# A scan-plus-FFN kernel on one core: the 64-bit weights' last bits copied as 16-bit words, and another order of work on ScalarE and SyncE

## The chip, the core and the metric

The program runs on one core of a Trainium2 chip. The core has five engines, each with its own in-order queue: TensorE (PE in the profile, its weight loads PEld), VectorE (DVE), ScalarE (ACT), GpSimd (POOL) and SyncE (SP), which here issues all DMAs. They wait for each other through semaphores. The metric is the device time of one execution in microseconds (us), lower is better.

## The reference

Two stages follow one another. The first is a chunked linear attention over 4 batches, 8 heads, 768 positions, head width 32 and state width 16; its result of 3072 tokens by 256 goes through a bilinear feed-forward stage:

```python
log_a = np.log(np.clip(a, 1e-06, 1.0))
for c in range(nc):
    cum = np.cumsum(la, axis=-1)
    L = np.exp(cum[:, :, :, None] - cum[:, :, None, :]) * causal
    M = np.einsum('bhin,bhjn->bhij', Cc, Bc) * L
    y = np.einsum('bhij,bhjd->bhid', M, xc) + np.einsum('bhin,bhnd->bhid', Cc, state) * np.exp(cum)[..., None]
    state = decay_full * state + np.sum(Bx, axis=2)
...
a = x @ w1
b = x @ w2
h = a * b @ w3
return (h @ w_out).astype(np.float32)
```

x, a, B and C are float32. The four weight matrices w1, w2 (256 x 1024), w3 (1024 x 1024) and w_out (1024 x 256) come as float64, and the kernel must turn them into float32 itself.

## The kernel before

**Tiling.** The 768 positions are cut into 16 chunks of 48 (c0 to c15) and 8 slabs of two chunks (0 to 7); a slab holds 2 x 48 positions of 4 batches, which is 384 tokens. A chunk's steps are: loads `.T`, `.X`, `.K` and `sN.N`; `D0`, `D1` (the exponents' differences as matrix products), `E0`, `E1` (exp on ACT), `B0`, `B1` (weighting B, on POOL), `C` (C times B, 16 products), `M0` to `M3` (times the decay, on DVE), `Y` (32 small products, output and new state), `Z` and `x0` to `x3` (the state is transposed and copied into the next chunk's operand XE), `h` (ACT writes the high part of the output into XT) and `l` (DVE writes the remainder). From chunk 2 on the differences need cumulative sums that are computed once, written to DRAM by `a.save` and read back by each chunk's `.K`.

**Feed-forward.** w3 and w_out are first multiplied with each other, so that only two products per slab remain. For slab s and column block f (0 to 7) `ls.f.0` and `ls.f.1` are the two products x w1 and x w2, six matmuls of 384 columns each. `ls.f.a` copies the first from its PSUM bank into the gate buffer (ACT), `ls.f.g` multiplies the second in (DVE), `ls.f.h` casts the product to its high part (ACT), and `ls.f.l` subtracts for the low part (POOL or DVE). `zs.0` to `zs.2` are the products down to 256 columns, 24 matmuls of 256 columns each, and `ys.k` copies them out (ACT), `ys.kd` stores them (SP). High and low parts live in the buffer G, a ring of 9 column blocks: a cast into a block waits until the products of the slab before have read it. G shares its memory with the words' buffers below, so no cast runs before the last weight word is used.

**Words.** A weight block w0 to w7 (w1 and w2), o0 to o3 (w_out), v0 to v15 (w3) takes these steps: `.D` loads 512 KB of float64 into `st` (4 buffers), `.A` scales the high word into `mag` (6 buffers), `.Y` copies the low word's top bits over the high word's last bits, which `.A` has already read, `.L` shifts those bits down and keeps them with the sign, `.S` shifts `mag` up and sets them in. For w blocks `.H` and `.P` split the result into a high and a low part, for v blocks `.M` multiplies it with w_out (8 matmul records), and `eN.a`, `eN.b` split the sum for a pair of column blocks.

**Order.** Nothing is scheduled by the compiler: the string PLAN names every step in program order, and each engine runs its own steps in that order. A letter behind a colon picks the engine (a, v or p). `+5` puts in five matmuls of zeros on PE, which compute nothing. Up to slab 2 the column products share three PSUM banks in turn (bank 4, 5, 6), from then on four (bank 4 to 7); `pl_bank` assigns them by the table ORDER, which the change leaves alone.

Of the kernel before, what the change touches and what calls it, by code (L numbers as in the profile page):

```python
# [30 lines left out]
k.I b.m01:v k.X c1.X b.m10:v c0.D0 b.m11:v w2.D k.L1 c0.D1 c0.E0 a.scan c2.T k.R0 a.t0:p w3.D c1.D0 c0.E1 a.r0:p  # L31
w0.A:a k.R1 c0.B0 c1.D1 s1.N c1.E0 c0.B1 c0.M0 c0.M1 c1.B0 c0.M2 c1.E1 c0.M3 w0.Y:v +1 c0.Y c1.B1 a.t1:p w0.L
c1.C a.r1:p c0.Z c0.x0:v c0.x1:a a.save c0.x2:v c0.x3:a c2.X c1.M0 c0.h c1.M1 c1.M2 w1.A:a c1.M3 w0.S +6 c1.Y
w1.Y:a w0.H:v w4.D w0.P:v c1.h c0.l w2.A:a c1.l +5 l0.0.0 w2.Y:a w1.L w1.S l0.0.1 c2.K w1.H:v l0.0.a w3.A:a
w1.P:v c3.T +1 l0.1.0 c3.X c1.Z w3.Y:a w2.L w5.D l0.1.1 w2.S c3.K c1.x0:a c1.x1:v c2.D0 c1.x2:a c1.x3:v c2.D1
w2.H:v c2.E0 w6.D w2.P:v c2.E1 c2.B0 l0.1.a c2.B1 +3 c2.C l0.0.g w4.A:a l0.2.0 c2.M0 w4.Y:a c2.M1 c2.M2 c2.M3
w3.L c2.Y w3.S l0.2.a w5.A:a l0.2.1 w3.H:v w7.D w5.Y:a w3.P:v c3.D0 c3.D1 c4.T l0.1.g l0.3.1 c4.K c2.Z c3.E0
w4.L c2.h c3.B0 l0.3.0 s2.N c3.E1 c2.l c4.X c2.x0:a c3.B1 w4.S c3.C c2.x1:a c2.x2:a c2.x3:v o0.D c3.M0 l0.3.a
c3.M1 w6.A:a c3.M2 c3.M3 w4.H:v c3.Y w6.Y:a w4.P:v l0.4.1 l0.2.g w7.A:a w5.L l0.4.0 w5.S w7.Y:a w5.H:v o1.D
c4.D0 c4.D1 w5.P:v c5.T l0.4.a c5.K o0.A:a l0.3.g l0.5.1 c3.Z o0.Y:a l0.4.g l0.5.0 c5.X w6.L w6.S c3.h l0.5.a  # L40
c3.l o2.D l1.0.0 w6.H:v o1.A:a w6.P:v l1.0.1 l1.0.a l0.5.g o1.Y:a l1.0.g l0.6.0 w7.L c4.E0 o0.L l0.6.1 l0.6.a
c4.B0 w7.S c4.E1 l1.1.0 w7.H:v o3.D o2.A:a c4.B1 o0.S w7.P:p o2.Y:a l1.1.1 l0.6.g v0.D o1.L l0.7.0 o1.S l1.1.a
c3.x0:a l1.1.g v1.D l0.7.1 l0.7.a o2.L c3.x1:a o2.S c3.x2:a l1.2.0 o3.A:a l0.7.g v2.D c3.x3:v l1.2.1 l1.2.a
o3.Y:v v0.A:a l1.3.0 o3.L v0.Y:v l1.3.1 l1.3.a v0.L v1.A:a v0.S c4.C v1.Y:a o3.S v4.D v0.M c4.M0 v3.D c4.M1
# [12 lines left out]
c7.M3 l2.5.1 l2.5.a e3.b c8.T l0.7.l:p l1.0.h c8.K c7.Y l2.5.g l1.0.l:p l2.6.0 c7.Z c7.x0:v c7.h c7.x1:v l2.6.1
l2.6.a c7.l c7.x2:a c7.x3:v l2.7.0 l2.6.g s4.N l2.7.1 l2.7.a c8.X z0.0 l2.7.g z0.1 y0.0 y0.0d c9.T c9.K z0.2
y0.1 l2.0.h y0.1d l1.1.h l2.0.l:p l1.2.h l1.1.l:v l1.3.h l1.2.l:p l1.4.h l1.3.l:v c8.D0 l1.5.h c8.D1 l1.4.l:p
l1.6.h l1.5.l:v l1.7.h l1.6.l:p y0.2 l1.7.l:v c9.X c8.E0 l3.0.0:4 c8.E1 y0.2d c8.B0 c8.B1 z1.0 l3.0.a z1.1 y1.0  # L60
y1.0d z1.2 y1.1 y1.1d l2.1.h l2.2.h l2.1.l:p l2.3.h l2.2.l:v l2.4.h l2.3.l:p l3.0.1:4 l2.4.l:v y1.2 l2.5.h y1.2d
l2.6.h l2.5.l:p c8.C l3.0.g l2.7.h l2.6.l:v l3.1.0:4 l3.0.h l2.7.l:p c8.M0 c8.M1 l3.1.1:4 c8.M2 l3.1.a l3.0.l:p
c8.M3 c10.T l3.2.0:4 l3.1.g c10.K l3.2.1:4 l3.2.a c8.Y l3.2.g l3.3.0:4 c8.Z c8.x0:v c8.h c8.x1:v s5.N l3.3.1:4
l3.3.a c8.l c8.x2:a c8.x3:v l3.4.0:4 l3.3.g c10.X c9.D0 c9.D1 c9.E0 l3.4.1:4 c9.E1 c9.B0 l3.4.a c9.B1 c9.C
l3.4.g l3.5.0:4 c9.M0 c9.M1 c9.M2 c9.M3 l3.5.1:4 l3.5.a c11.T l3.6.0:4 l3.5.g c11.K l3.6.1:4 l3.6.a c9.Y l3.6.g
l3.7.0:4 c9.Z c9.x0:v c9.h c9.x1:v l3.7.1:4 l3.7.a c9.l c9.x2:a c9.x3:v z2.0 l3.7.g c11.X z2.1 y2.0 y2.0d z2.2
y2.1 y2.1d l3.1.h l3.2.h l3.1.l:p l3.3.h l3.2.l:v l3.4.h l3.3.l:p l4.0.0:4 l3.4.l:v y2.2 l3.5.h y2.2d l3.5.l:p
c10.D0 l4.0.a c10.D1 l4.0.1:4 c10.E0 c10.E1 c10.B0 l3.6.h c10.B1 c10.C l4.0.g l3.7.h l3.6.l:p l4.1.0:4 c10.M0
# [24 lines left out]
"""


@with_exitstack
def kernel(
    ctx: ExitStack,
    tc: tile.TileContext,
# [21 lines left out]
    nc = tc.nc  # L121
# [29 lines left out]
    def ins(i):  # L151
        return tc.keep_in_program_order(i) if ordered[0] else i
# [298 lines left out]
    def from_f64(name, loads, dst=None):  # L451
# [5 lines left out]
        v = {}  # L457
# [18 lines left out]

        @task(name + ".Y")
        def _(e):
            b = v["st"].bitcast(U8).rearrange("p (k e) -> p k e", e=8)
            copy(e, b[:, :, 4], b[:, :, 3])  # L480

        @task(name + ".L")
        def _(e):
            w = v["wh"].bitcast(I32)
            ins(nc.vector.tensor_scalar(w, w, 5, 7 - 2 ** 31, ALU.arith_shift_right, ALU.bitwise_and))  # L485
# [210 lines left out]
```

## Time and profile before

| | us |
|---|---|
| device time, median of 3 runs | 299.51 (299.01 to 301.11) |
| profiled execution, device time | 297.72 |
| profiled execution, span on the core | 296.0 |
| mean granted TensorE clock | 0.994 |
| DVE busy (317 instructions) | 155.5 |
| ACT busy (280) | 145.5 |
| POOL busy (105) | 68.6 |

Busy times overlap, so they say how much an engine did and not what the end waits for. PE is busy through nearly the whole span, so what counts is where PE stands still. The span has these stages: up to about 18 us the first loads and chunks 0 and 1; to 58 us the conversion of w1, w2 and w_out beside slab 0 and the first columns of slab 1; to 117 us the w3 blocks and the columns of slabs 1 and 2; at 116.8 us the first product down, z0; from then on, slab after slab, columns and products down. In the timelines the tile names are those of the code without their buffer numbers.

### The profile page before, as it was taken

Reading aid. Unit: us, or ns where it says so; the run is one execution under the profiler, and the core shown is the slowest. Engines: PE = TensorE matmul, PEld = TensorE weight load, DVE = VectorE, ACT = ScalarE, POOL = GpSimd, SP = SyncE. Lnnn points to the kernel's source line nnn. Section 1 sums busy time; section 2 is a strip of 40 time slices with the busy share of each in tenths; the row PEclk is TensorE's granted clock in tenths of the full one; section 3 lists DMA queues with packets and bytes.
Section 4 is the critical chain, followed back from the end, with each engine's and each line's share of the span. In section 5 each row is a group of like instructions: output and inputs, shape, how many; then the busy total and the mean of one; then the engine's idle time right before and its main releaser. Section 6 shows DMA issues by size and latency. Waiting matters only on the chain.

```text
span 296.0 us, 7543 instructions
## 1 busy us (share of the span) xinstructions
PE 281.7 (95%) x3076; PEld 254.3 (86%) x3080; DVE 155.5 (53%) x317; ACT 145.5 (49%) x280; POOL 68.6 (23%) x105
## 2 busy tenths in 40 slices
PE   8979869999999999959999999999999999999994
PEld 3467769888998999959999999999999999999994
DVE  4789959898775264062654355435543552332040
ACT  4589868688775283163442444244424441442241
POOL 8501003010001073082410341034103410340060
PEclk9999999999999999979999999999999999999999
DMA  5987865759881000311320132113211000100021
GB/s 160 332 230 232 217 219 166 251 169 295 282 268 49 27 2 2 89 39 38 102 73 29 41 97 77 29 38 99 76 29 37 20 2 2 35 20 0 18 56 36
DMA packets 22818, 29.47 MB, mean 100 GB/s; under 512 B 5530, under 2 KB 13056, under 8 KB 22784
## 3 DMA queue, kind: packets, MB, share of 16 engines
q1 hardware_dynamic: 22784, 29.00, 33.3%
q8 instruction: 24, 0.39, 0.6%
q14 instruction: 10, 0.08, 0.1%
HBM read 25.54 MB, written 3.29 MB: 97 GB/s over the span
## 4 chain that ended last, share of the span: by engine, by line
PE 89%; ACT 4%; DMA 2%; issue 1%; POOL 1%; DVE 1%; POOLq 0%; ACTq 0%; DVEq 0%
PE bank L155 89%; DMA st<-in_w_out_dram 2%; ACT g L161 1%; ACT st L161 1%; POOL g L164 1%; ACT mag L472 0%; POOLq L691 0%; ACT rr L387 0%; ACT xe L161 0%; DVE mag L491 0%; ACT ob L161 0%; ACT gf L161 0%; DVE st L485 0%; DVE rr L164 0%; ACT xt L161 0%
## 5 line engine op out<-in xcount | busy, mean ns | idle before, releaser
L155 PE MATMUL bank<-xt,w 128*128 128x384 f32 x768 | 148.6, 344 | 6.2 <-ACT ob L161 3.4
L155 PEld LDWEIGHTS bank<-xt,w 128*128 128x128 f32 x768 | 133.1, 189 | 11.2 <-ACT ob L161 3.7
L155 PE MATMUL bank<-woh,g 128*128 128x256 f32 x384 | 69.7, 281 | 0.3 <-POOL g L164 0.3
L164 POOL TENSOR_TENSOR g<-gf,g 128x384 fp32r<-128x384 f32 x40 | 44.1, 1124 | 110.7 <-PE bank L155 50.7
L164 DVE TENSOR_TENSOR gf<-gf,bank 128x384 f32<-128x384 f32 x64 | 35.3, 552 | 51.5 <-PE bank L155 43.3
L155 PEld LDWEIGHTS bank<-woh,g 128*128 128x128 f32 x384 | 59.6, 189 | 0.5 <-POOL g L164 0.5
L164 DVE TENSOR_TENSOR g<-gf,g 128x384 fp32r<-128x384 f32 x24 | 27.3, 1169 | 52.1 <-PE bank L155 30.7
L155 PE MATMUL bank<-wol,g 128*128 128x256 f32 x192 | 53.8, 280 | 0.0
L161 ACT COPY gf<-bank 128x384 f32<-128x384 f32 x64 | 31.4, 491 | 41.9 <-PE bank L155 41.7
L164 POOL TENSOR_TENSOR rr<-bn,rr 128x128 f32<-128x128 f32 x32 | 14.2, 458 | 105.0 <-ACT rr L387 62.9
L155 PEld LDWEIGHTS bank<-wol,g 128*128 128x128 f32 x192 | 36.4, 189 | 0.0
L161 ACT COPY ob<-bank 128x256 f32<-128x256 f32 x24 | 8.9, 372 | 50.8 <-PE bank L155 35.8
L161 ACT CAST g<-gf 128x384 fp32r<-128x384 f32 x64 | 29.0, 515 | 7.1 <-PE bank L155 6.4
L161 ACT COPY st<-st 128x512 uint8<-128x512 uint8 x22 | 30.3, 1376 | 0.6
L155 PE MATMUL bank<-wof,mag 128*128 128x256 f32 x128 | 29.7, 381 | 0.3 <-issue 0.2
L155 PEld LDWEIGHTS bank<-wof,mag 128*128 128x128 f32 x128 | 24.0, 190 | 3.5 <-DVE mag L491 0.4
L472 ACT ACTIVATE mag<-st 128x512 f32<-128x512 f32 x27 | 18.6, 688 | 10.0 <-DMA st<-in_w3t_dram 5.3
L155 PEld LDWEIGHTS bank<-rr,xe 64*32 64x32 f32 x1024 | 15.4, 107 | 7.3 <-issue 4.6
L155 PE MATMUL bank<-rr,xe 64*32 64x64 f32 x1024 | 18.5, 218 | 2.2 <-issue 1.5
L164 DVE TENSOR_TENSOR rr<-bank,rr 128x192 f32<-128x192 f32 x64 | 18.4, 349 | 2.0 <-POOL rr L164 1.5
L161 ACT CAST xt<-bank 128x384 fp32r<-128x384 f32 x16 | 7.8, 489 | 23.4 <-DVE zz L430 20.7
L387 ACT ACTIVATE rr<-bank 128x384 f32<-128x384 f32 x32 | 14.7, 502 | 8.6 <-PE bank L155 8.5
(57 smaller groups left out, 150.5 us busy)
## 6 DMA issues: line engine op xcount, KB each, us to landing
st<-in_w3t_dram SPq DMA_DIRECT2D x16, 512.0 KB
st<-in_w_dram SPq DMA_DIRECT2D x16, 256.0 KB
xe<-in_x_dram SPq DMA_DIRECT2D x32, 96.0 KB
bc<-in_Bt_dram SPq DMA_DIRECT2D x8, 320.0 KB
bc<-in_Ct_dram SPq DMA_DIRECT2D x8, 320.0 KB
bn<-in_Bn_dram SPq DMA_DIRECT2D x8, 256.0 KB
st<-in_w_out_dram SPq DMA_DIRECT2D x4, 512.0 KB
out_dram<-ob SPq DMA_DIRECT2D x16, 96.0 KB
```

Source lines behind the costliest of these rows:

```text
L155: return tc.keep_in_program_order(nc.tensor.matmul(*args, **kw))
L161: return ins(nc.scalar.copy(*args) if eng == "a" else {"v": nc.vector, "p": nc.gpsimd}[eng].tensor_copy(*args))
L164: return ins({"v": nc.vector, "p": nc.gpsimd}[eng].tensor_tensor(*args))
L387: ins(nc.scalar.activation(R[:, hf * G8:(hf + 1) * G8, N:], v["pd", hf], AF.Exp))
L472: ins(nc.scalar.activation(v["mag"], v["wh"], AF.Copy, scale=2.0 ** -112))
```

## The change

`.Y` copies one uint16 of each pair of words in place of one uint8, so 16 bits are put into the high word in place of 8, and `.L` shifts by 13 in place of 5. The counts of these copies per engine go from 22 on ACT and 6 on DVE to 21 and 7. Everything else is another PLAN:

- w_out's first scaling `o0.A` stands on ACT behind chunk 3's `h`, in place of ahead of it; blocks w4 to w7 and chunks 2 to 5 are interleaved otherwise.
- Chunk 2's loads `c2.X` go out on SP ahead of `c2.T` and `w3.D`, in place of behind `a.save`; `o0.D` goes out ahead of `s2.N` and `c4.X`; after z0 the stores `y0.0d` and `y0.1d` stand ahead of `c9.T`.
- `w4.P` moves from DVE to POOL, `o3.A` and `v13.A` to DVE, `v12.A` to ACT; the state copies on ACT go from 21 to 24.
- The casts of slab 1 (`l1.1.h` to `l1.7.h`) stand ahead of `l2.0.h`, in place of behind it. `z1.0` to `z1.2` follow on `c8.D1` at once, and `l3.0.0` comes behind them. In later slabs the fifth column's cast stands ahead of the last copy out of the product down (`y2.2` and so on) in place of behind it.
- The zero matmuls are 29 in place of 28 (`+4` ahead of c2's `D0` in place of `+3` behind its `D1`).

```diff
-U8 = mybir.dt.uint8
+U16 = mybir.dt.uint16
...
-y0.1 l2.0.h y0.1d l1.1.h l2.0.l:p l1.2.h l1.1.l:v l1.3.h l1.2.l:p l1.4.h l1.3.l:v c8.D0 l1.5.h c8.D1 l1.4.l:p
+z0.2 y0.1 l1.1.h y0.1d l1.2.h l1.1.l:p c9.T l1.3.h l1.2.l:v c9.K l1.4.h l1.3.l:p l1.5.h l1.4.l:v c8.D0 l1.6.h
...
-            b = v["st"].bitcast(U8).rearrange("p (k e) -> p k e", e=8)
-            copy(e, b[:, :, 4], b[:, :, 3])
+            b = v["st"].bitcast(U16).rearrange("p (k e) -> p k e", e=4)
+            copy(e, b[:, :, 2], b[:, :, 1])
...
-            ins(nc.vector.tensor_scalar(w, w, 5, 7 - 2 ** 31, ALU.arith_shift_right, ALU.bitwise_and))
+            ins(nc.vector.tensor_scalar(w, w, 13, 7 - 2 ** 31, ALU.arith_shift_right, ALU.bitwise_and))
```

Three places show how the order moves. First ACT around the first w_out block. Before, from `l0.4.a` on: `gf<-bank6` is `l0.4.a`, the next two rows are `o0.A` and `o0.Y`, `xt<-bank3` is `c3.h`, then `l0.5.a`, `o1.A`, `l1.0.a`.

```order
L161 COPY gf_67<-bank6_83 128x384
L472 ACTIVATE mag_89<-st_88 128x512
L161 COPY st_88<-st_88 128x512
L161 CAST xt_68<-bank3_80 128x8x48
L161 COPY gf_67<-bank5_82 128x384
L472 ACTIVATE mag_89<-st_88 128x512
L161 COPY gf_67<-bank4_81 128x384
```

The same place now, from `l0.4.a` to `o0.Y`; the two rr rows are `c4.E0` and `c4.E1`, the xe row is `c3.x0`.

```order
L161 COPY gf_67<-bank6_83 128x384
L387 ACTIVATE rr_70<-bank0_77 128x8x48
L387 ACTIVATE rr_70<-bank1_78 128x8x48
L161 CAST xt_68<-bank3_80 128x8x48
L161 COPY xe_69<-zz_73 16x8x32
L161 COPY gf_67<-bank5_82 128x384
L472 ACTIVATE mag_89<-st_88 128x512
L161 COPY gf_67<-bank4_81 128x384
L161 COPY st_88<-st_88 128x512
```

`o0.A` has moved behind `c3.h` and `l0.5.a`, and `o0.Y` behind `l1.0.a`.

Second, PE behind `z0.2` (the last row on bank6 that reads G), before: `c8.D0`, `c8.D1`, then `l3.0.0`, then `z1.0` on bank7.

```order
L155 MATMUL bank6_83<-woh_64,g_1207 128x256
L155 LDWEIGHTS ld_90
L155 MATMUL bank0_77<-rd_91,ld_90 128x384
L155 LDWEIGHTS ld_90
L155 MATMUL bank1_78<-rd_91,ld_90 128x384
L155 MATMUL bank6_83<-xt_68,w12_63 128x384 x6
L155 MATMUL bank7_84<-woh_64,g_1207 128x256
```

Now, with the same names:

```order
L155 MATMUL bank6_83<-woh_64,g_1208 128x256
L155 LDWEIGHTS ld_90
L155 MATMUL bank0_77<-rd_91,ld_90 128x384
L155 LDWEIGHTS ld_90
L155 MATMUL bank1_78<-rd_91,ld_90 128x384
L155 MATMUL bank7_84<-woh_64,g_1208 128x256
```

`l3.0.0` no longer stands between chunk 8's `D1` and `z1.0`; it writes the bank that `z0.2` used.

Third, SP early, before: from `w2.D` over `c2.T` (bc), `w3.D`, `k.R1` (rd), `s1.N` (bn), `a.save` (cd) and `c2.X` (xe) to the first of `c2.K`.

```order
L158 DMA bc_72<-in_Bt_dram 128x640
L158 DMA st_88<-in_w1_dram 128x2x256
L158 DMA st_88<-in_w2_dram 128x2x256
L158 DMA rd_91<-rd_91 102x768
L158 DMA bn_71<-in_Bn_dram 128x512
L158 DMA cd_99<-gf_67 128x576
L158 DMA xe_69<-in_x_dram 48x512 x2
L158 DMA st_88<-in_w1_dram 128x2x256
L158 DMA st_88<-in_w2_dram 128x2x256
L158 DMA ld_90<-cd_99 48x2x48
```

The same stretch now:

```order
L158 DMA xe_69<-in_x_dram 48x512 x2
L158 DMA bc_72<-in_Bt_dram 128x640
L158 DMA st_88<-in_w1_dram 128x2x256
L158 DMA st_88<-in_w2_dram 128x2x256
L158 DMA rd_91<-rd_91 102x768
L158 DMA bn_71<-in_Bn_dram 128x512
L158 DMA cd_99<-gf_67 128x576
L158 DMA st_88<-in_w1_dram 128x2x256
L158 DMA st_88<-in_w2_dram 128x2x256
L158 DMA ld_90<-cd_99 48x2x48
```

Chunk 2's x rows stand first; `a.save` has two more DMAs ahead of it, and `c2.K`, which waits for it, keeps its place behind `w4.D`.

More of the change, by code (lines that the diff above doesn't have):

```diff
@@ L30 @@
 k.z b.D k.q b.tab a.D c0.T s0.N k.p c0.X w0.D b.clip a.clip b.ln a.ln k.r b.m00:v c1.T a.exp w1.D k.L0 +12 c0.C
[L31 to L44, printed above, removed]
```

108 lines of the change are left out of this document (61 added, 47 removed).

## The prediction

> **What bounds the kernel now.** I read the page's head first, then the busy time by stage (columns: stretch, its length, then busy time and instructions of PE, PEld, DVE, ACT and POOL, granted clock, DMA share, GB/s), then the chain of work that ended last.
>
> ```profile
> span 296.0 us, 7543 instructions
> 18.40:41.33 22.93, 19.57 (x277) 16.12 (x275) 19.17 (x44) 19.36 (x31) 1.62 (x4) 1.00 0.79 226
> 41.33:58.16 16.83, 16.53 (x176) 15.24 (x177) 15.48 (x31) 13.27 (x22) 2.54 (x3) 1.00 0.59 188
> 58.16:116.80 58.64, 58.64 (x562) 52.19 (x563) 39.17 (x83) 38.55 (x62) 10.46 (x13) 1.00 0.47 145
> 125.27:134.55 9.28, 5.93 (x35) 5.54 (x34) 4.91 (x4) 4.92 (x12) 5.92 (x6) 0.82 0.13 36
> 134.55:280.15 145.60, 145.60 (x1642) 138.30 (x1641) 60.98 (x123) 53.74 (x124) 32.52 (x39) 1.00 0.16 44
> ...
> 32.37 6.46 DMA st<-in_w_out_dram
> 38.91 0.67 ACT mag L472
> 39.60 1.35 ACT st L161
> 40.96 0.33 ACT xt L161
> ```
>
> PE is the bound: it is busy for all of 58.16 to 116.80 and all of 134.55 to 280.15. Only where it stands idle can a new order gain: 22.93 - 19.57 = 3.36 us up to 41.33, 0.30 up to 58.16, 9.28 - 5.93 = 3.35 behind z0, where the clock is down to 0.82 too, and at the end, where the order is the same as before. The chain names the first: o0's data land at 38.83, then `o0.A` and `o0.Y` run on ACT, and only then `c3.h`, for which PE waits.
>
> **Behind z0.** These rows are ACT and PEld behind z0.2, then what prices PE's work (a stretch of three column products, one of a product down, a chunk's D0 and D1 with what follows them), then the last slab, whose order is already what the change makes of slab 1: ACT, POOL and DVE around z7.0, and z7.0 itself.
>
> ```profile
> 125.41 3.40 ACT L161 CAST g<-gf 128x384 fp32r<-128x384 f32 x8 [2.39 <-PE bank L155]
> 128.72 0.36 ACT L161 COPY ob<-bank 128x256 f32<-128x256 f32 x1
> 129.13 1.78 PEld L155 LDWEIGHTS bank<-xt,w 128*128 128x128 f32 x6 [3.74 <-ACT ob L161]
> 50.13:53.25 3.12, 3.12 (x20) 3.12 (x20) 3.02 (x6) 2.29 (x5) 0.00 (x0) 1.00 0.78 244
> 122.45:125.27 2.82, 2.82 (x26) 2.78 (x25) 0.00 (x0) 0.37 (x1) 0.00 (x0) 1.00 0.52 147
> ...
> 23.00 0.50 PE L155 MATMUL bank<-rd,ld 102*128 102x384 bf16 x2
> 23.34 0.81 PE L155 MATMUL bank<-zero 128*128 128x512 bf16 x3
> ...
> 280.35 0.37 ACT L161 COPY ob<-bank 128x256 f32<-128x256 f32 x1 [2.41 <-PE bank L155]
> 280.62 3.00 ACT L161 CAST g<-gf 128x384 fp32r<-128x384 f32 x7
> 281.21 4.93 POOL L164 TENSOR_TENSOR g<-gf,g 128x384 fp32r<-128x384 f32 x4 [18.76 <-ACT g L161]
> 281.58 3.68 DVE L164 TENSOR_TENSOR g<-gf,g 128x384 fp32r<-128x384 f32 x3 [6.26 <-ACT g L161]
> L164 POOL TENSOR_TENSOR g<-gf,g x4: 1027/1341/1355, 281.2 to 284.8; 128x384 fp32r<-128x384 f32 x4
> 282.98:286.42 3.44, 3.18 (x26) 2.98 (x25) 2.29 (x2) 0.91 (x3) 3.17 (x3) 1.00 0.14 39
> ```
>
> Before, eight casts start at 125.41, when z0.2 is through, because the first of them, `l2.0.h`, writes the ring's block that z0.2 reads last. The copy out of z0.2's bank stands behind them, and `l3.0.0` needs that bank: PEld waits 3.74 us. Between 125.27 and 134.55 PE does D0, D1, l3.0.0 and z1.0. Now `l1.1.h` leads, whose block z0.2 reads first; in the last slab the same order lets the casts start at 280.62, while z6.2 still runs. There z7.0 takes 3.44 us in place of 2.82, since PE reaches the late columns before their subtractions are done: 0.62 lost. Slab 1 has D0 and D1 in between, 0.34 us for such a pair (23.00 to 23.34), so 0.62 - 0.34 = 0.28 stays. The new stretch holds 0.34 + 1.04 (3.12 / 3) + 2.82 + 0.28 = 4.48 us, against 9.28: **-4.8 us**. The bounds: -5.1 with no wait left, -4.2 with the last slab's 0.62 and a further 0.3. Late next are slab 2's casts beside and behind z1.2, which z2.0 wants only behind slab 3's sixteen column products, 16.6 us of PE; and l3.0.0's bank is free by then, its copy having had z1's 8.5 us. Moving the fifth column's cast ahead of `y2.2` and its like delays one bank by a cast, 0.43 us (3.00 / 7); three column products, over 3.1 us, pass before that bank is written again, so it costs nothing. The stores and `c9` loads that change places on SP serve work in the last stretch of the first fence, where PE never waits.
>
> **The early stages.** These are PE's waits from 30 us on, then SP's issues around `c2.X`, then PE at c0.Y and at its last small product of c1.Y, ACT at `w3.A`, and the price of the `.P` subtraction on POOL and on DVE.
>
> ```profile
> 32.01 1.51 PE L155 MATMUL bank<-rr,xe 64*32 64x64 f32 x64 [0.59 <-ACT gf L161]
> 36.42 2.36 PE L155 MATMUL bank<-xt,w 128*128 128x384 f32 x12 [0.23 <-ACT gf L161]
> 41.33 0.45 PE L155 MATMUL bank<-xt,w 128*128 128x384 f32 x1 [2.55 <-ACT xt L161]
> ...
> 10.29 0.35 SPq L158 DMA_DIRECT2D bc<-in_Bt_dram  x1
> 14.61 0.36 SPq L158 DMA_DIRECT2D cd<-gf  x1
> 15.07 1.67 SPq L158 DMA_DIRECT2D xe<-in_x_dram  x2
> 19.27 0.34 SPq L158 DMA_DIRECT2D ld<-cd  x1
> 19.67 0.64 SPq L158 DMA_DIRECT2D rd<-cd  x2
> ...
> 11.47 1.10 PE L155 MATMUL bank<-rr,xe 64*32 64x64 f32 x64
> 17.32 0.24 PE L155 MATMUL bank<-rr,xe 64*32 64x64 f32 x1 [1.50 <-issue]
> ...
> 20.29 0.68 ACT L472 ACTIVATE mag<-st 128x512 f32<-128x512 f32 x1
> ...
> L164 POOL TENSOR_TENSOR w<-mag,w 128x512 fp32r<-128x512 f32 x1 | 1.7, 1679 | 0.4 <-DVE w L161 0.4
> L164 DVE TENSOR_TENSOR w<-mag,w 128x512 fp32r<-128x512 f32 x7 | 4.8, 692 | 0.2
> ```
>
> *What goes.* With `o0.A` behind `c3.h` and `l0.5.a`, the 2.55 us before l1.0.0 go: behind c3.Y only c4's two exps stand ahead of `c3.h`, and `c3.l` on DVE, late next, is wanted by the fifth of l1.0.0's six matmuls alone. The 0.59 and 0.23 come from ACT doing three state copies and w6, w7 in a row; these are spread now. With the 0.30 that makes 3.67.
>
> *What comes.* `c2.X` overwrites x rows that c0.Y reads until 11.47 + 1.10 = 12.57, and now stands at the head of SP's queue, so `c2.T` (10.29 before), w3, `k.R1`, `s1.N` and `a.save` queue behind that wait. From 12.6 the issues ahead of `a.save` take some 3.2 us (the rows show 0.35 to 0.45 each), so it goes out at about 15.8 in place of 14.61. `c2.K` followed it by 19.27 - 14.61 = 4.66, and c2's D0 ran at most 23.00 - 19.67 = 3.33 after the last of `c2.K`: D0 is ready by 24.2. PE comes there at 23.00 + 4 x 0.27 (0.81 / 3) = 24.1 (both rows in the fence before). I charge the one zero matmul more and the remainder: 0.5. w3 goes out up to 3 us later than before and is used on ACT at 20.29, so it is covered; w4's cover is thinner. `w4.P` on POOL takes 1.68 in place of 0.69, and l0.4.1 follows closer than before: 1.0 more, of which half lies beside chunk 3's D products: 0.5. The 1.50 of the "issue" row at 17.32 stays, since PE's own order there is the same. Sum: -3.67 + 0.5 + 0.5 = **-2.7 us**, with ends at 0 (every wait returns elsewhere) and -3.7 - 0.8 (nothing returns, and waits hidden inside busy PE shrink too).
>
> **The word copies.** These rows group the copies and their neighbours (count, then busy, mean ns).
>
> ```profile
> L161 ACT COPY st<-st 128x512 uint8<-128x512 uint8 x22 | 30.3, 1376 | 0.6
> L472 ACT ACTIVATE mag<-st 128x512 f32<-128x512 f32 x27 | 18.6, 688 | 10.0 <-DMA st<-in_w3t_dram 5.3
> L161 DVE COPY st<-st 128x512 uint8<-128x512 uint8 x6 | 4.5, 746 | 1.1 <-ACT mag L472 0.9
> L485 DVE TENSOR_SCALAR st<-st 128x512 int32<-128x512 int32 x28 | 12.3, 447 | 6.6 <-ACT st L161 6.4
> ```
>
> No uint16 copy is in the trace. On ACT it lies between 0.69 (a word per element with the same step) and 1.38 (as the bytes); on DVE between 0.45 and 0.75. On both engines bytes cost about twice a whole word, so I take 0.69 and 0.45, the rows of the wider type. ACT is then freed of 30.3 - 21 x 0.69 = 15.8 us. Almost none of it is on the path: in 58.16 to 116.80, where most copies run, PE waits for nothing, and before 58 the remaining waits hang on loads, DVE and POOL. I credit 0.1 us; the bounds are +0.5 (at 1.38 the copies in the new ACT order hold `c2.E1` and `w4` up) and -0.7. The shift by 13 is the instruction it was.
>
> The Trainium skill, "ScalarE: Activation LUTs", section "What ACT_TABLE_LOAD costs", gives 186 ns + 0.833 ns per element whatever the type named there, an estimate of 0.61 us for 512; the byte row at 1.376 contradicts it, so it does not remove the chance that uint16 is slow as well. By it the sum would be as mine.
>
> **The sum.** -4.8 - 2.7 - 0.1 = -7.6 us. Against the profiled execution (297.72, span 296.0) that gives 290.1. The timed runs lie higher, median 299.51, lowest 299.01; since the change will be timed like those, I take the lowest: 299.01 - 7.6 = **291.4 us**.
>
> **The rivals.**
> 1. *The early part is paid back.* SP's queue behind `c2.X` runs later than I think and c2's D0, w4 or w5 make PE wait for what the other moves save. For it: DMA share 0.79 in that stage, no slack. Only -4.8 is left, less a little: 294.5.
> 2. *uint16 copies as slow as bytes.* The change's first part then does nothing on ACT. For it: the row with bytes breaks with the other types. Price +0.5: 291.9.
> 3. *More gain.* Words come early, no wait returns, hidden waits shrink: -5.1 - 4.5 = -9.6, 289.4; at most 288.
> 4. *The subtractions exclude each other.* If POOL and DVE took turns at them, seven of 1.03 us (the shortest, 1027 ns) would end 7.2 us after the first cast and z1.0 would wait about 2.4 us: 293.8. Against it: in the last slab four on POOL take 4.93 and three on DVE 3.68 of the same time. The Trainium skill, "SBUF — State Buffer", section "SBUF: two separate sides", calls the shared pair an exclusive lock for such a pair of operations; the trace disagrees in that both went on, at 1.3 in place of 1.03 each.
> 5. *Slower.* `c2.K` waits for a write to DRAM and stands in line behind everything on SP. If w3, `a.save` and `w4.D` piled up so that c2's D0 came after 32 us in place of 24, the early part would cost 8 us and eat all: 299.5 and above. Nothing in the rows gives more than 1 to 2 us.
>
> **How the numbers follow.** Forecast 0.52; rival 1 0.18; rival 2 0.13; rival 3 0.10; rival 4 0.03; rival 5 0.02; the rest, 0.02, anywhere. The time is that of the forecast, 291.4. The range takes rival 3's far end, 288.0, and reaches past rival 1 for the spread of single runs (299.01 to 301.11): 295.2. 1% of 299.51 is 3.0 us, about what a measurement of this kernel can tell. Faster than 296.5: forecast, rivals 2, 3, 4 and nearly all of 1, 0.94. Within 1%: 0.04. Slower: 0.02.
>
> **What would show it.** Right: z1.0 starts within 0.5 us of c8's D1, takes about 3.1 us, and the clock stays at 1.00 there; no PE wait over 1 us before l1.0.0, which starts near 38.6; ACT's copies on st at 0.7 us, ACT busy down by some 15 us with PE's stage from 58 to z0 unchanged in length. Wrong: a wait of PE at c2's D0 above 1 us, casts that start only when z0.2 has ended, or a new idle stretch of PE in the w3 stage because a block comes late.

## The result, and the profile after

| | before | after |
|---|---|---|
| device time, median of 4 runs | 300.06 us (299.01 to 301.11) | 290.77 us (290.57 to 292.98) |
| profiled execution, device time and span | 297.72, 296.0 | 292.98, 291.3 |
| mean granted TensorE clock of the profiled execution | 0.994 | 0.991 |
| the same, of the changed kernel's other four timed executions | | 1.0 each |

The ratio is 0.9708, 95% interval [0.9657, 0.9759]: faster, by 9.3 us between the medians, against the forecast 291.4 and the range 288.0 to 295.2. Ratios, here and below, are taken over the runs within 1.5% of the fastest of their kernel, which drops some runs of the kernel before in the experiments; where that matters the medians of all runs stand beside them.

The changed kernel's profiled execution is its slowest of five: 292.98 us. First its head and the shares of its chain, then its stages (columns: stretch, its length, busy time and instructions of PE, PEld, DVE, ACT, POOL, then granted clock, DMA share, GB/s).

```profile
span 291.3 us, 7557 instructions
PE 88%; DMA 3%; issue 2%; SPq 2%; POOL 2%; DVE 2%; POOLq 0%; ACT 0%; ACTq 0%; DVEq 0%
```

```profile
22.90:24.49 1.59, 0.00 (x1) 0.03 (x1) 1.52 (x4) 1.53 (x4) 0.00 (x0) 1.00 0.36 41
24.49:36.87 12.38, 10.26 (x168) 8.29 (x168) 7.89 (x21) 8.86 (x15) 2.89 (x5) 1.00 0.88 273
36.87:40.28 3.41, 3.41 (x71) 2.84 (x70) 3.16 (x7) 2.44 (x5) 0.41 (x1) 0.50 0.34 115
58.16:116.91 58.75, 58.75 (x562) 51.97 (x561) 40.07 (x84) 39.89 (x66) 9.96 (x13) 1.00 0.51 154
125.39:128.96 3.57, 3.34 (x29) 3.08 (x27) 3.57 (x3) 2.21 (x6) 3.57 (x4) 1.00 0.61 166
```

```profile
123.16 3.00 ACT L161 CAST g<-gf 128x384 fp32r<-128x384 f32 x7
```

The casts of slab 1 now start at 123.16, while z0.2 still runs. Behind z0 the stretch from chunk 8's `D0` to the end of `z1.0` is 3.57 us at full clock; with `l3.0.0`, which now runs later and takes 1.04, that is 4.61 in place of 9.28. The early stages look as if nothing had been gained: z0 starts at 116.91, before at 116.80. But 3.41 us of them, from 36.87 on, ran at half clock, which the other executions of the changed kernel did not do. These are PE's waits ahead of that stretch and SP's issues.

```profile
24.49 0.48 PE L155 MATMUL bank<-rd,ld 102*128 102x384 bf16 x2 [1.59 <-DMA rd<-cd]
...
34.73 0.58 PE L155 MATMUL bank<-bc 32*64 32x96 f32 x30 [1.37 <-DVE xt L164]
35.74 1.41 PE L155 MATMUL bank<-xt,w 128*128 128x384 f32 x6 [0.43 <-DVE gf L164]
...
12.68 1.96 SPq L158 DMA_DIRECT2D xe<-in_x_dram  x2
...
17.66 0.37 SPq L158 DMA_DIRECT2D cd<-gf  x1
18.13 1.96 SPq L158 DMA_DIRECT2D st<-in_w_dram  x2
22.07 0.34 SPq L158 DMA_DIRECT2D ld<-cd  x1
```

`c2.X` waits for c0.Y as predicted, but `a.save` goes out at 17.66, not 15.8, and PE waits 1.59 us at c2's `D0`. The 1.37 us are chunk 3's `C`: one of its banks still holds chunk 2's output until `c2.l` on DVE (the last row) has read it. `c2.l` waits for the cast `c2.h` on ACT (the row at 33.63), and that stands behind `w6.A`, which waits for w6's data:

```profile
32.68 0.67 ACT L472 ACTIVATE mag<-st 128x512 f32<-128x512 f32 x1 [0.99 <-DMA st<-in_w_dram]
33.26 0.46 ACT L387 ACTIVATE rr<-bank 128x384 f32<-128x384 f32 x1
33.63 0.46 ACT L161 CAST xt<-bank 128x384 fp32r<-128x384 f32 x1
33.99 0.49 ACT L387 ACTIVATE rr<-bank 128x384 f32<-128x384 f32 x1
...
34.12 0.56 DVE L164 TENSOR_TENSOR xt<-bank,xt 128x384 fp32r<-128x384 f32 x1 [1.89 <-ACT xt L161]
```

Last, the word copies, grouped (count, busy, mean ns): the row with uint8 has become a row with uint16, with one copy fewer and the same price.

```profile
L161 ACT COPY st<-st 128x512 uint16<-128x512 uint16 x21 | 28.9, 1375 | 0.6
```

### The profile page after: what moved, and what is told of

Same layout as the page of the kernel before. It is cut to its first block, busy times and chain, and to the rows that moved or that the text cites. A ratio compares the mean times of both kernels' runs of the same rounds, so it can differ in the third digit from the quotient of the medians.

```text
span 291.3 us, 7557 instructions
## 1 busy us (share of the span) xinstructions
PE 282.0 (97%) x3081; PEld 253.8 (87%) x3081; DVE 156.2 (54%) x315; ACT 144.4 (50%) x281; POOL 71.1 (24%) x106
## 4 chain that ended last, share of the span: by engine, by line
PE 88%; DMA 3%; issue 2%; SPq 2%; POOL 2%; DVE 2%; POOLq 0%; ACT 0%; ACTq 0%; DVEq 0%
PE bank L155 88%; DMA st<-in_w_dram 2%; SPq L158 2%; POOL g L164 2%; DMA cd<-gf 1%; POOLq L691 0%; DVE rr L164 0%; DVE w L164 0%; DVE xe L161 0%; DVE mag L491 0%; DVE gf L164 0%; ACT xt L161 0%; DVE w L161 0%; ACT ob L161 0%; DVE zero L261 0%
## 5 line engine op out<-in xcount | busy, mean ns | idle before, releaser
L164 POOL TENSOR_TENSOR g<-gf,g 128x384 fp32r<-128x384 f32 x40 | 45.4, 1159 | 103.7 <-ACT g L161 56.4
L155 PEld LDWEIGHTS bank<-woh,g 128*128 128x128 f32 x384 | 59.0, 187 | 1.0 <-POOL g L164 0.9
L164 DVE TENSOR_TENSOR g<-gf,g 128x384 fp32r<-128x384 f32 x24 | 28.9, 1247 | 46.4 <-ACT g L161 25.5
L161 ACT COPY st<-st 128x512 uint16<-128x512 uint16 x21 | 28.9, 1375 | 0.6
L472 ACT ACTIVATE mag<-st 128x512 f32<-128x512 f32 x26 | 17.9, 695 | 4.3 <-DMA st<-in_w_dram 3.5
```

Of the source, the lines that this page charges most:

```text
L155: return tc.keep_in_program_order(nc.tensor.matmul(*args, **kw))
L161: return ins(nc.scalar.copy(*args) if eng == "a" else {"v": nc.vector, "p": nc.gpsimd}[eng].tensor_copy(*args))
L164: return ins({"v": nc.vector, "p": nc.gpsimd}[eng].tensor_tensor(*args))
L472: ins(nc.scalar.activation(v["mag"], v["wh"], AF.Copy, scale=2.0 ** -112))
```

## The experiments

In the diffs a line is a stretch of PLAN. "Clock loss" is one minus the mean granted clock, times the span, averaged over a kernel's runs; the span less its clock loss is called full-clock time, and given as a median. Over the 51 executions of the kernel before that were timed beside the experiments it is 3.2 us; in the changed kernel's five executions it is 0.5. One stretch of 3.41 us at half clock costs 1.7 us and shows as a mean clock of 0.994. The loss includes up to 0.9 us of a stretch that begins behind PE's last product and costs nothing, so it is good to some tenths. The diffs of the kernels called "the kernel before with" are against that one, the others against the changed kernel.

**The late half alone** (the kernel before with the new order from z0.0 on):

```diff
-z0.0 l2.7.g z0.1 y0.0 y0.0d c9.T c9.K z0.2 y0.1 l2.0.h y0.1d l1.1.h l2.0.l:p l1.2.h
+z0.0 l2.7.g z0.1 y0.0 y0.0d z0.2 y0.1 l1.1.h y0.1d l1.2.h l1.1.l:p c9.T l1.3.h l1.2.l:v
...
```

> The kernel before up to z0.0, with byte copies, and the changed order from z0.0 on. Theory (the order behind z0 is worth 4.7 us, as the two profiles show: 9.28 us between z0.2 and the end of z1.0 against 4.6, less nothing given back later): 300.06 - 4.7 = 295.4 us, 294.9 to 295.9, clock 1.00 behind z0. Rival one (the early part was paid back in full, as in the profiled execution of the changed kernel, and all 9.3 us come from z0 on): 290.8. Rival two (part of the 4.7 comes back as waits of z2.0 for casts): 297 or more.

292.4 us (291.05 to 294.17) beside 299.17, ratio 0.9776 [0.9718, 0.9834]: 6.8 gained, more than the 4.7 I expected and less than all. Of it 2.2 us are clock: loss 1.1 against 3.2 beside it. In its profile the stretch behind z0 is 3.55 us.

**The early half alone** (the new order up to z0.0, uint16 copies, then the old order):

```diff
-z0.0 l2.7.g s4.N c8.X z0.1 y0.0 y0.0d z0.2 y0.1 l1.1.h
+s4.N c8.X z0.0 l2.7.g z0.1 y0.0 y0.0d c9.T c9.K z0.2 y0.1 l2.0.h
...
```

> The changed kernel up to z0.0, with uint16 copies, and the order of the kernel before from z0.0 on. Theory (what the order behind z0 does not give comes from the stages ahead of 58 us): 300.06 - 4.6 = 295.5 us, 295.0 to 296.2, in a profile l1.0.0 near 38 to 39.5 us in place of 41.33. My prediction's term of 2.7 would give 297.4. Rival one (the early part is paid back): 299.5 to 300.5, l1.0.0 after 41.

296.59 us (9 runs, 294.21 to 297.54), ratio 0.9952 [0.9902, 1.0002]: 2.6 between the medians, my predicted 2.7 and less than the 4.6 that I had come to expect from the result. Its clock loss is 3.1 us. The same early part with the new late order loses 0.5, so about 2.6 of it belongs to the old order behind z0; one such stretch is in its profile (127.96 on), and where a second one lies in the six runs with a mean clock under 0.99 no profile shows. By the ratio the early half gains only 1.4, and its interval reaches 1, so from these times alone a gain is not clear of the noise; its profile, where z0 starts at 114.57 in place of 116.80, shows 2.2. The two halves together, 6.8 + 2.6 = 9.4, make the whole; by the ratios they make 0.9776 x 0.9952 = 0.9729, which is what the changed order with byte copies has beside the same runs (below).

**Behind z0: which of the two moves.** Casts first as changed, but `l3.0.0` ahead of `z1.0` again:

```diff
-y0.2 l1.7.l:p z1.0 c8.E0
+y0.2 l1.7.l:p l3.0.0:4 z1.0 c8.E0
...
-l2.4.l:v l3.0.0:4 y1.2
+l2.4.l:v y1.2
```

> The changed kernel with l3.0.0 between c8's D1 and z1.0 again, the casts of slab 1 first as changed. Theory (the order of the casts carries the gain behind z0: y0.2 follows them by 0.4 us after z0.2's end, l3.0.0 then covers what z1.0 waits for its last subtractions): 0.0 to +0.4 against the changed kernel, 290.8 to 291.3, clock 1.00 there. Rival (the product at once carries it: l3.0.0 waits for the bank and z1.0 moves out): +1.5 or more, 292.3 and above, an idle stretch of PE over 1 us behind c8's D1.

292.22 us (291.46 to 294.16), ratio 0.978 [0.9714, 0.9846]: 1.4 above the changed kernel, more than the 0.4 that I allowed, and close to the rival's 1.5. Of it 0.6 is clock (loss 1.1; the half-clock stretch in its profile starts at 36.54, far ahead of this place), and PE's wait for the bank, over 1 us for the rival, is 0.6. And `z1.0` at once as changed, but the casts behind `l2.0.h` again:

```diff
-y0.1 l1.1.h y0.1d l1.2.h l1.1.l:p
+y0.1 l2.0.h l1.1.h y0.1d l2.0.l:v l1.2.h l1.1.l:p
...
-c8.B0 l2.0.h c8.B1 l2.0.l:v z1.1
+c8.B0 c8.B1 z1.1
```

> The changed kernel with the casts of slab 1 behind l2.0.h again, z1.0 directly behind c8's D1 as changed. Theory (the casts start only when z0.2 has read its last block, at its end; eight of 0.43 and the subtractions behind them hold z1.0's last columns up to about 6 us behind z0.2's end, in place of 3.6, and the idle stretch brings a clock drop of 1.7 us): +2.4 to +4.2, 293.2 to 295.0. Rival (z1.0 at once carries the gain): within 0.5 of the changed kernel, 290.3 to 291.3.

293.6 us (292.75 to 294.36), ratio 0.9842 [0.9784, 0.9901], 2.8 above the changed kernel, but without the clock drop that my expectation held in its upper part. The stretch from D0 to the end of z1.0, with `l3.0.0` in it in the first kernel and not in the second, and the second kernel's ACT:

```profile
125.90:130.99 5.09, 4.50 (x35) 4.12 (x33) 3.69 (x3) 2.21 (x6) 4.33 (x5) 1.00 0.48 134
```

```profile
122.58:128.94 6.36, 4.66 (x29) 3.60 (x28) 4.25 (x4) 4.44 (x11) 5.17 (x5) 1.00 0.34 94
```

```profile
122.71 3.41 ACT L161 CAST g<-gf 128x384 fp32r<-128x384 f32 x8 [2.39 <-PE bank L155]
```

The casts start again only when z0.2 is through. With `l3.0.0` counted in (1.04 where it runs later) the four combinations are: casts late and l3.0.0 first 9.28, casts late and z1.0 first 7.40, casts first and l3.0.0 first 5.09, both moves 4.61. The 9.28 hold a half-clock stretch and the other three do not; the same order at full clock took 7.83 (the kernel with zero matmuls, below). So the casts carry 2.7 to 2.8 us, `z1.0` at once 0.4 to 0.5, in either order, and 1.4 or 1.5 of the 4.67 are clock.

**The clock.** The kernel before, with zero matmuls inside PE's two long waits:

```diff
-c3.h l0.5.a c3.l o2.D l1.0.0
+c3.h l0.5.a c3.l o2.D +8 l1.0.0
...
-c8.D0 l1.5.h c8.D1 l1.4.l:p
+c8.D0 l1.5.h c8.D1 +12 l1.4.l:p
```

> The kernel before with 8 zero matmuls ahead of l1.0.0 and 12 behind c8's D1, which run inside PE's two long waits; no wait goes. Theory (a long wait of PE costs twice: its own time, and 3.4 us at half clock, 1.7 us, when it falls so that PE idles half of one 3.4 us stretch; of the 9.3 us gained by the change some 3.4 are clock, the mean granted clock of before being 0.98 to 0.994): granted clock 0.994 to 1.00 in the runs, 1.00 behind z0, time 2 to 3.4 us under before, 295.8 to 297.2 beside 299.2. Rival (the clock follows the waits but costs nothing that the waits don't hide, or the fills delay PE): within 1 us of before or slower.

296.64 us (12 runs) beside 299.12 (17 runs), ratio 0.9958 [0.9917, 0.9999]; clock loss 0.9 against 3.7, or 2.9 over the runs that the ratio takes. Work that computes nothing gains 2.5 us between the medians, 1.2 by the ratio, whose interval all but reaches 1: the drop in clock loss is plain, the gain in time only just clear of the noise. Full-clock time is nearly the same, 293.9 against 294.2. This is PE behind z0 there, with the stretch from `D0` to the end of z1.0:

```profile
124.89 0.50 PE L155 MATMUL bank<-rd,ld 102*128 102x384 bf16 x2
125.23 2.75 PE L155 MATMUL bank<-zero 128*128 128x512 bf16 x12
128.75 1.31 PE L155 MATMUL bank<-xt,w 128*128 128x384 f32 x6 [0.77 <-ACT ob L161]
...
124.89:132.72 7.83, 7.07 (x46) 5.26 (x45) 4.92 (x4) 4.91 (x12) 5.93 (x6) 1.00 0.17 45
```

The wait for the bank lasts as long as ever (3.86 us behind `D0`, before 129.13 - 125.27 = 3.86), but `z1.0` follows 1.15 us behind `l3.0.0`'s start, where at half clock it took 2.09. So a wait can be paid for twice.

**Early: `c2.X`.** Behind `a.save` again:

```diff
-c0.Z c2.X c0.x0:v
+c0.Z c0.x0:v
...
-c1.Y s1.N w1.Y:a a.save w0.H:v
+c1.Y s1.N w1.Y:a a.save c2.X w0.H:v
```

> The changed kernel with c2.X behind a.save on SP again. Theory (c2.X at the head of SP's queue holds a.save and with it c2.K, c2's D0 and later loads up by some 3 us, of which PE saw 1.6 at c2's D0 in the profile): a.save near 14.6, no wait of PE over 0.3 at c2's D0, 289.3 us, 288.6 to 290.0. Rival one (the wait only moves on to w5, w6 and o0, whose data are late by the load on the DMA engines): 290.4 to 291.2. Rival two (c2.X late makes c2.Y or the x rows late): 291.5 or more.

290.92 us (289.4 to 291.47), ratio 0.9715 [0.9665, 0.9765]: the same as the changed kernel. It is the time of rival one, and not for its reason: the wait at c2's D0 is gone, the full-clock time is 287.1 against 288.9, but the clock loss is 1.8 against 0.5. The two nearly cancel. What came back is PE's wait inside `c1.Y` for its own instructions. These are that kernel's PE at c1.Y, and the same place in the changed order (from the kernel with byte copies, below):

```profile
14.63 1.30 PE L155 MATMUL bank<-rr,xe 64*32 64x64 f32 x63
17.19 0.24 PE L155 MATMUL bank<-rr,xe 64*32 64x64 f32 x1 [1.27 <-issue]
```

```profile
14.62 1.30 PE L155 MATMUL bank<-rr,xe 64*32 64x64 f32 x63
16.09 0.24 PE L155 MATMUL bank<-rr,xe 64*32 64x64 f32 x1 [0.17 <-issue]
```

With the old order on SP, w3's load in flight ahead of c1.Y, that wait is 1.27 to 2.41 us in all five profiles (1.50 in the kernel before); in the seven with `c2.X` at the head none is over 0.25. Each kernel has a single profile; how the wait comes about is taken up in the last section. The other way to mend c2's D0 is to put all that `c2.K` needs ahead of `c2.X`, and w3 behind:

```diff
-a.scan k.R0
+a.scan c2.T k.R0
...
-c0.Z c2.X c0.x0:v c0.x1:a c2.T c0.x2:v
+c0.Z k.R1 s1.N a.save c2.X c0.x0:v c0.x1:a c0.x2:v
...
-c1.M3 k.R1 w0.S +6 c1.Y s1.N w1.Y:a a.save w0.H:v
+c1.M3 w0.S +6 c1.Y w1.Y:a w0.H:v
```

> The changed kernel with c2.T, k.R1, s1.N and a.save ahead of c2.X on SP, and w3.D behind them, so that no weight block is loaded while PE fetches its instructions at c1.Y. Theory (two effects were in conflict: w3's load ahead of c1.Y costs PE about 1.3 us in its instruction fetch, and a.save behind c2.X costs 1.6 us at c2's D0): a.save near 13.6, wait at c1.Y under 0.5, wait at c2's D0 under 0.3, l1.0.0 near 38: 289.4 us, 288.8 to 290.2, clock 1.00. Rival one (what c2's D0 gains is lost again at w3 to w6, whose loads come no earlier): 290.4 to 291.0. Rival two (the fetch stall comes from the number of transfers in flight, whatever they are, and returns): as the kernel with c2.X alone moved back, 290.9.

289.77 us (289.68 to 290.5), ratio 0.972 [0.9677, 0.9763], clock loss 0.2: 1.0 under the changed kernel between the medians, the lowest of all, but by the ratio (0.9708 for the changed kernel) no gain shows. `a.save` goes out at 13.30, c2's D0 waits for nothing, the wait in c1.Y is 0.64, a little over the 0.5 expected. PE next waits 0.86 us behind c2's D1 for a bank that `l0.1.a` frees late. That copy moved ahead as well (the diff is against this kernel):

```diff
-w2.L c1.x0:a c3.T l0.1.1 w2.S c1.x1:a c3.X c1.x2:a c1.x3:v l0.1.a
+w2.L l0.1.a c1.x0:a c3.T l0.1.1 w2.S c1.x1:a c3.X c1.x2:a c1.x3:v
```

> The kernel with a.save first on SP (289.77) with l0.1.a ahead of chunk 1's state copies on ACT, too. Theory (in that kernel PE waits 0.86 us behind c2's D1 for a bank that l0.1.a frees late, since w3's data hold ACT up; with the copy first that wait goes and nothing else takes its place): 288.9 us, 288.5 to 289.3, no wait of PE over 0.3 behind c2's D1. Rival (PE then waits at c2's C or at l0.4.1 for the state copies or chunk 2's exps instead): 289.5 to 290.0.

290.29 us (289.32 to 292.4), beside 296.94 for the kernel before, ratio 0.9777 [0.9733, 0.9821]: a miss. The wait is gone, and full-clock time is the same as without the move (287.8 and 287.9). Two of the six runs have a mean clock of 0.991; in the profiled one of them a half-clock stretch follows on a wait of 1.86 us in c1.Y, which had been 0.64 with the same order on SP. That wait differs from execution to execution.

**Early: `o0.A`.** In the changed kernel, ahead of chunk 3's `h` again:

```diff
-l0.4.g c3.h c3.x0:a
+l0.4.g o0.A:a o0.Y:a c3.h c3.x0:a
...
-c5.X o0.A:a w6.S
+c5.X w6.S
...
-o2.D o0.Y:a w6.P:v
+o2.D w6.P:v
```

> The changed kernel with o0.A and o0.Y ahead of chunk 3's h on ACT again. Theory (the wait of 2.55 us before l1.0.0 came from these two, which wait for o0's data and then take 0.69 and 1.38): a wait of PE of 2 to 2.6 us before l1.0.0 returns, +2.0 to +2.6 us, and in some runs 1.7 us of half clock more: 292.8 to 294.5. Rival (the wait went because chunk 3 runs earlier or o0's data come earlier, not because of these two): within 0.7 of the changed kernel.

292.45 us (292.08 to 293.41), ratio 0.9837 [0.9783, 0.989]: 1.7 above the changed kernel, under the 2.0 to 2.6 expected and above the rival's 0.7; 0.6 of it is clock. The kernel before ran lower beside it, 296.94 (11 runs), and by the ratios the loss is 3.9 us, so its size is uncertain; that the move costs something is clear in both. In its profile the early part was already late by a half-clock stretch, and l1.0.0 still waits 0.69 us for `c3.h`. The other test is the kernel before with this move and the late half, and nothing else of the change (the late half is not shown again):

```diff
-l0.4.a c5.K o0.A:a l0.3.g l0.5.1 c3.Z o0.Y:a l0.4.g
+l0.4.a c5.K l0.3.g l0.5.1 c3.Z l0.4.g
...
-c3.h l0.5.a c3.l o2.D l1.0.0 w6.H:v o1.A:a w6.P:v l1.0.1 l1.0.a l0.5.g
+c3.h l0.5.a o0.A:a c3.l o2.D l1.0.0 w6.H:v w6.P:v l1.0.1 l1.0.a o0.Y:a o1.A:a l0.5.g
```

> The kernel before with the changed order from z0.0 on and, of the early part, only o0.A behind l0.5.a, o0.Y behind l1.0.a and o1.A behind that; byte copies, c2.X behind a.save, chunks and blocks interleaved as before. Theory (two local moves hold the gain; the rest of the new order nets nothing, since what it saves at c1.Y it loses at c2's D0): the wait before l1.0.0 is under 0.5 us, 1.5 to 2.5 under the kernel with the late order alone (292.4), so 290.0 to 291.2, the changed kernel's time. Rival (the wait of l1.0.0 comes back as a wait for o0's and o1's words or at the columns behind, and the rest of the new order is what gains): 291.8 or more.

292.79 us (292.39 to 295.43), ratio 0.9827 [0.9776, 0.9878]: my theory fell. The wait before l1.0.0 is gone, and yet the kernel is no faster than the late half alone (292.4). Its PE waits, summed (us in total, times, longest):

```profile
PE bank L155 <- issue: 2.4, 1, 2.4
PE bank L155 <- DVE zero L261: 1.3, 1, 1.3
PE bank L155 <- ACT gf L161: 0.8, 2, 0.6
PE bank L155 <- POOL w L164: 0.6, 1, 0.6
```

2.4 us are c1.Y's instruction wait, 0.6 a new wait behind l1.0.0, for a subtraction on POOL. From l1.0.0 (39.76) to z0.0 (116.31) PE takes 76.55 us, before 75.47: 1.1 of the 2.55 are given back there. The changed kernel is 2.0 us faster than this one, and their intervals do not meet, so the rest of the early order, chunks and blocks interleaved otherwise, is worth something; which part of it, no run shows.

**The copies.** The changed kernel with bytes again:

```diff
-            b = v["st"].bitcast(U16).rearrange("p (k e) -> p k e", e=4)
-            copy(e, b[:, :, 2], b[:, :, 1])
+            b = v["st"].bitcast(U8).rearrange("p (k e) -> p k e", e=8)
+            copy(e, b[:, :, 4], b[:, :, 3])
...
-            ins(nc.vector.tensor_scalar(w, w, 13, 7 - 2 ** 31, ALU.arith_shift_right, ALU.bitwise_and))
+            ins(nc.vector.tensor_scalar(w, w, 5, 7 - 2 ** 31, ALU.arith_shift_right, ALU.bitwise_and))
```

> The changed kernel with the byte copies and the shift by 5 of the kernel before, same order. Theory (a uint16 copy takes what a byte copy takes, 1.375 against 1.376 us on ACT and some 0.75 on DVE): 290.8 us, 290.4 to 291.2, the copies' rows again 1.38 and 0.75. Rival (the 16-bit copies help somewhere that the rows don't show, by memory traffic): 291.5 or more.

291.0 us (290.49 to 291.87), ratio 0.9729 [0.9683, 0.9775]: 0.2 us from the changed kernel, within the noise, so the type is worth nothing that these runs can tell. Its profile (span 289.2, clock 1.0) is the changed order in an execution without a half-clock stretch, and the one to read the early part from: its stages from c1.Y's end, and PE's wait at chunk 3's `C`.

```profile
17.17:23.02 5.85, 5.85 (x31) 4.53 (x29) 5.62 (x13) 5.62 (x9) 0.00 (x0) 1.00 0.86 267
23.02:24.66 1.64, 0.00 (x1) 0.03 (x1) 1.57 (x4) 1.07 (x2) 0.00 (x0) 1.00 0.40 42
24.66:39.80 15.14, 14.19 (x246) 11.54 (x247) 11.55 (x29) 11.81 (x20) 3.67 (x7) 1.00 0.84 266
39.80:114.68 74.88, 74.81 (x738) 67.41 (x739) 54.01 (x113) 52.12 (x84) 11.63 (x14) 1.00 0.52 163
```

```profile
33.76 0.58 PE L155 MATMUL bank<-bc 32*64 32x96 f32 x30 [0.48 <-DVE xt L164]
```

What sets a copy's price was measured by itself, ten forms behind the last copy out:

```diff
+    for eng in "av":
+        for _ in range(2):
+            copy(eng, dst, two[:, :, 1])
+            copy(eng, two[:, :, 1], dst)
...
+            copy(eng, h4[:, :, 2], h4[:, :, 1])
+            copy(eng, dst.bitcast(U16)[:, 0:512], h4[:, :, 1])
+            copy(eng, h4[:, :, 2], dst.bitcast(U16)[:, 0:512])
+            copy(eng, dst.bitcast(U16)[:, 0:512], src.bitcast(U16)[:, 0:512])
+            copy(eng, h2[:, :, 1], h2[:, :, 0])
...
```

> The changed kernel with ten forms of a 128x512 copy, twice each, first on ACT and then on DVE, behind the last copy out, on the gate buffer; nothing reads their results and the time tells nothing. In order: words at every second word to contiguous; contiguous to every second word; every second word in place; contiguous words; uint16 as the last bits' copy (8 byte step in and out); uint16 8 byte step to contiguous; uint16 contiguous to 8 byte step; uint16 contiguous; uint16 at every second half word in place; uint8 as before. Theory (an engine writes narrow elements that don't fill a word slowly: the price lies in the write of parts of words): ACT 0.69 for the words and for uint16 to contiguous, 1.38 wherever single uint16 or uint8 are written with a step; DVE 0.45 and 0.75. Rival (the price lies in the type alone): all uint16 and uint8 forms 1.38 on ACT. Second rival (it lies in the step of the output, whatever the type): words to every second word 1.38 as well, contiguous uint16 0.69.

On ACT, in order: words to every second word, uint16 with a step of 8 bytes in and out, step in only, step out only, contiguous, and step 4 in and out.

```profile
287.93 0.65 ACT L161 COPY gf<-gf 128x512 f32<-128x512 f32 x1
...
289.93 1.35 ACT L161 COPY gf<-gf 128x512 uint16<-128x512 uint16 x1
291.00 0.71 ACT L161 COPY gf<-gf 128x512 uint16<-128x512 uint16 x1
291.74 1.32 ACT L161 COPY gf<-gf 128x512 uint16<-128x512 uint16 x1
293.10 0.62 ACT L161 COPY gf<-gf 128x512 uint16<-128x512 uint16 x1
293.74 0.76 ACT L161 COPY gf<-gf 128x512 uint16<-128x512 uint16 x1
```

The price lies in the write: single half words at every eighth byte cost twice, whether they are read with a step or not; whole words at the same step, and half words read with it, do not. On DVE the five uint16 forms take 0.74, 0.45, 0.73, 0.29 and 0.45, the words 0.43: there too the write at every eighth byte is the expensive one, but a step on the reading side alone costs as well, 0.45 against 0.29. The theory holds but for one point: half words at every fourth byte, which don't fill a word either, cost 0.76 on ACT and not 1.38.

## Why the prediction came out as it did

- **z0 transition, -4.8.** Right in mechanism and size: -4.67 between the profiles (9.28 to 4.61; predicted 4.48 left), mostly by the casts. `z1.0` starts at D1's heels, takes 3.37 us at full clock like the last slab's 3.44, and the casts start at 123.16 while z0.2 runs. Two small terms were off and nearly cancel: D0 and D1 take 0.20 us and not 0.34, and so `z1.0`'s wait for its last subtractions is 0.55 (3.37 - 2.82) and not 0.28. In the timed runs the old order behind z0 lost about 2.6 us of clock by the early-half kernel, not the one stretch of 1.7 in the profile that I counted.
- **Early stages, -2.7.** The sum was near, -2.1 (z0 starts at 114.68 in place of 116.80) to -2.6 (early half, between the medians; 1.4 by the ratio), and this was luck, since three of its terms were wrong. Of my signs of being wrong two came true, a wait over 1 us at c2's D0 and a new idle stretch, and l1.0.0 starts at 39.80 (with byte copies) in place of 38.6. *"The 1.50 of the "issue" row at 17.32 stays, since PE's own order there is the same"* failed: it went to 0.17, with the order on SP and not PE's own. The 0.5 for c2's D0 was 1.9 (1.64 of wait and 0.27 for the zero matmul): D0 came at 24.49 to 24.66, close to the 24.2 I had worked out, but PE was there at 22.90 and not at 24.1, having not waited in c1.Y. The two errors, 1.3 and 1.4, happen to cancel. I had `a.save` at 15.8; it was 17.66, because the issues ahead of it took 5.0 us and not 3.2: I took 0.35 to 0.45 for each DMA, where `c2.X` alone took 1.96 for its two, and a row of my own showed 1.67 for them. The 0.5 for `w4.P` on POOL did not appear: `l0.4.1` waits 0.26 us, for an ACT copy. Not foreseen at all was the wait at chunk 3's `C`, 0.48 us with w6's data there in time and 1.37 with them late: the "new idle stretch" of my list, one stage earlier than the w3 stage that I named. The 2.55 us before l1.0.0 went; moved alone they come back by nearly half behind it.
- **Word copies, 0.1.** The step that failed is *"On both engines bytes cost about twice a whole word, so I take 0.69 and 0.45, the rows of the wider type"*: 1.375 and 0.75, rival 2's premise. ACT's busy time is 144.4, not 15 us lower. In the sum the step was worth only 0.1, since ACT is off the path where most copies run; what quick copies would have gained, and so rival 2's price of 0.5, stays open, since no kernel here had them in this order.
- **The base.** I set the sum against the lowest timed run, 299.01, without asking why timed runs lie 1.3 to 3.4 us above the profiled one. Most likely it is the clock: the clocks of those runs are not on record, but in the 51 executions beside the experiments 3.2 us were lost on average, and 1.7 in the profiled one. Against the 0.5 after, 2.7 of the gain is clock, and my sum had 1.7 of that, as part of the z0 term. In full-clock time the gain is 5.0 us (293.9 before over the 51, 288.9 after) where my terms come to 7.6 - 1.7 = 5.9. So I overrated the waits by 0.9 and underrated the clock by 1.0. What is left between 9.3 and 5.0 + 2.7 lies within the scatter of the kernel before, whose runs beside the experiments ranged from 295.38 to 303.58. That the forecast came within 0.6 us of the time is luck in part: the two errors of this paragraph cancel too.
- **The rivals.** Rival 1, the early part paid back, is true of the changed kernel's profiled execution alone, by a half-clock stretch. Rival 2's premise came true, and the time, 290.77, lies under its 291.9. Rivals 4 and 5 did not happen. Seven subtractions of 1.03 us in turn would have ended 7.2 us after the first began, at 131.0, and `z1.0` was through at 128.96; whether POOL and DVE share or alternate in shorter turns the rows do not tell. c2's D0 came at 24.5.

## What to carry to other kernels

Price a long wait of TensorE twice: for its length, and for the half-clock stretch that it may set off, which shows in the granted clock of the timed runs and not in every profile. Ahead of a long product down, order casts by the ring's first free block, so that they run while the product before still reads its last ones. Copying half words in place of bytes gained nothing here, where each is written alone at every eighth byte; look at the write's step before counting on the type.

## What the runs showed of the hardware

**The clock drops on a grid.** In the fourteen profiled executions there are eight half-clock stretches ahead of the last instructions, each 3.41 us long. Within a run each starts a whole number of 3.413 us ahead of the stretch that follows the end of PE's work (49, 74, 80, 49, 75, 75, 77 and 79 times). The grid stretches ahead of them held 1.40 to 3.13 us of PE idle; others with up to 1.69 us passed, so the border is not sharp by this measure. It depends on a wait's place in the grid: the 2.55 us before l1.0.0 in the profile before, cut into 1.38 and 1.17 by it, cost no clock, while 1.84 us in c1.Y in the late-half kernel did.

```profile
14.60:18.01 3.41, 1.39 (x46) 1.00 (x44) 2.14 (x5) 1.88 (x3) 0.00 (x0) 1.00 0.86 254
18.01:21.42 3.41, 3.41 (x11) 3.00 (x10) 3.31 (x7) 2.25 (x3) 0.00 (x0) 0.50 0.97 286
```

These are two neighbouring grid stretches of the kernel with `l0.1.a` first: PE busy for 1.39 of 3.41 us, then half clock. The Trainium skill, "TensorE: Matmul & The Clock Gate", section "What's actually happening", gives a free-running window of 3413 ns, and half rate after at least one idle window; the runs agree on the window and disagree on the rest, since less than half a window of idle time was enough once (1.40 us).

**An instruction fetch can hold TensorE.** The wait named "issue" in c1.Y was 0.17 to 2.41 us with the same instructions on PE, by what SP had in flight: from 15 to 16 us the DMA share was 0.88 in the kernel before and 0.51 in the changed kernel with byte copies. The DMA records show what PE waits for. In all eight profiles with such a wait over 0.2 us, PE goes on 1.23 to 1.45 us behind the landing of one packet of 16 KB on the queue of the kind `instruction` (q8, 24 packets in an execution); in the kernel before it lands at 15.89, and PE goes on at 17.32. The packet itself takes 0.9 to 1.25 us in all fourteen profiles, but it starts at 14.70 to 15.96 with the old order on SP, at 12.61 to 13.56 with `c2.X` at the head, and in between (13.81 and 14.55) with `a.save` first. So the fetch is late and not slow, and not for PE's sake, which reaches c1.Y at 14.62 and 14.63 in the two views above. That it queues behind the weight load is argued from this; that the order on SP changes it is shown by moving `c2.X` alone.
